# A fused attention and expert kernel: the expert layers issued in one planned order of all engines, with float32 chunks first

## The chip, the cores and the metric

The kernel runs on one core of one Trainium2 chip. The metric is the device time of one execution in microseconds (us), as the median of several runs. PE is the matrix engine (TensorE), PEld its weight loads, DVE is VectorE, ACT is ScalarE, POOL is GpSimd, and SP issues most of the DMAs.

## What is computed

Causal attention over 8 batches x 12 heads x 448 positions x 64, whose result is read as 3584 tokens of 768 numbers, and then a layer of 8 experts of which each token takes one. An expert keeps the 80 tokens with the largest gate weight; all other rows of the result are zero.

```python
def _moe_ref(x, w_gate, w1, w2, capacity):        # x (3584, 768), w1 (8, 768, 1024), w2 (8, 1024, 768)
    ...
    for e in range(E):
        ...
            keep = np.argpartition(-gw, capacity)[:capacity]
            tok_idx = tok_idx[keep]
        h = np.maximum(x[tok_idx] @ w1[e], 0.0)
        out[tok_idx] = gate_w[tok_idx, None] * (h @ w2[e])
```

## The kernel before

The first 310 us are attention, 48 pairs of heads one after another. Then comes the **tail**: the last pair, the gate of the last batch and the choice of the 80 tokens of each expert. Its steps are issued in the order of the string `TAIL`. It ends with `idx` (the rows of the chosen tokens) and `gws` (their weights) on DVE (`finish`, L956 to L969).

Then come the experts, `e` from 0 to 7. Each has two layers, and the layers of neighbours alternate: e0 layer 1, e1 layer 1, e0 layer 2, e2 layer 1, e1 layer 2, and so on. The work on one expert:

- `gather` (POOL, L1259, an indirect DMA) brings 80 rows of the attention result from `xs` in HBM into `xg`. The rows were put there by stores from `xrl` (SP, L641), the last eight of them in the tail.
- `inputs`: PE transposes `xg` into `xtp` (L1273). ACT makes the float16 high part `xh` (L1281), DVE the low part `xl` (L1282).
- The weights are loaded in **pieces** of 1.5 MB into ten buffers, `wraw`, by SP. A piece holds three **chunks** of layer 1 (128 x 1024 each) or four of layer 2 (128 x 768). 112 chunks make the 32 pieces. Ten pieces are loaded during attention, 22 later, chunk by chunk (L223).
- Each chunk is **split**: ACT makes `wh` (L1235), DVE makes `wl` = 32 w - `wh` (L1221). There are 12 buffers of `wh` and 11 of `wl`. PE then needs three float16 matmuls for each block of 128 outputs (L1303, L1305, L1306; `product`). Some chunks are left whole, in float32, with one matmul for a block (L1296): those for which `whole` is true, three in layer 1 of e0 and otherwise the last chunk of each layer, none in e6 and e7. 98 chunks are split.
- `hidden` makes `hh` (ACT) and `hl` (DVE) from layer 1's result `hp`; `outputs` copies layer 2's result `op` to `yt`, transposes it (`ytp`, PE), scales it to `yo` (ACT) and **scatters** it to `out` (POOL, L1384, an indirect DMA). A scatter waits for the one before it.

What sets the order: only PE's is the order of the code, in which the product of a whole chunk comes last in its layer (`u.order`). The order on DVE, ACT, POOL and SP is made by the framework's own scheduler from what each instruction waits for. Some waits are added by hand: no `wl` before a small memset behind the first gather (L1418) or, in later ones, before the newest `xl` (`low_after`); loads are paced by the `wl` (`PACE`).

```python
        def low(l, src, h):
            with tc.issue_after((low_after or last_of)[-1].ins):
                return nc.vector.scalar_tensor_tensor(out=l, in0=src, scalar=SW, in1=h, op0=ALU.mult, op1=ALU.subtract)
...
                        with tc.issue_after(g.ins):
                            nc.gpsimd.memset(lows[0][0][:, 0:1], 0.0)
```

Of the kernel before, what the change touches and what calls it, by code (L numbers as in the profile page):

```python
# [17 lines left out]
P = 128  # L18
# [20 lines left out]
ta ya tb yb td guard yd tc yc invert last_rows v0 v1 gA vy sA gB0 w close piece lpA r0w wy lgA r0e gB1 logA r0m r1w sB r1e  # L39
# [5 lines left out]
ROW_ENGINES = "ppappppa"  # L45


@with_exitstack
def attention_then_moe(
# [84 lines left out]
    prob = [akeep.tile([P, at], F32, name=f"prob{r}") for r in range(2)]  # L134


    HB = 3
    PH = NP // HB
    v_bufs = []
    for r in range(2):  # L140
        t = akeep.tile([P, NT, PH * P], F32, name=f"vt{r}")
        if LAST < P:
            nc.gpsimd.memset(t[0:LAST, NT - 1, :], 0.0)
        v_bufs.append(t)
# [12 lines left out]
    flipped = []  # L157
    for r in range(2):
        t = akeep.tile([P, 2, WPT], F32, name=f"PT{r}")
        flipped.append(t)  # L160
# [17 lines left out]
    PACE = 1.28  # L178

    PW = 3072
    K1, K2 = PW // F, PW // D
    PIECES = []
    for e in range(E + 1):
        if e < E:
            PIECES += [(e, 1, c, K1) for c in range(0, NC1, K1)]
        if e:
            PIECES += [(e - 1, 2, c, K2) for c in range(0, NC2, K2)]
# [9 lines left out]
    def piece():  # L199

        e, which, c, k = PIECES[len(wload)]
        x = len(wload) % (WBUF + WMORE)
        pool, bufs = (wpool, WBUF) if x < WBUF else (wmore[0], WEARLY) if x < WBUF + WEARLY else (wmore[1], WMORE - WEARLY)
        t = pool.tile([P, k, PW // k], F32, name="wraw", tag="w", bufs=bufs)
        wload.append(t)
        return t, (w1 if which == 1 else w2)[e, :, c:c + k, :]

    lows_of = []

    def load_piece(behind=None, paced=False):  # L210

        if len(wload) < len(PIECES):
            late = len(wload) - WBUF - WMORE
            t, src = piece()
            if behind is not None:
                with tc.issue_after(behind.ins):
                    nc.gpsimd.memset(t[:, 0, 0:1], 0.0)
            if not paced:
                nc.sync.dma_start(t, src)
                return  # L220
            k = t.shape[1]
            for j in range(k):
                got = nc.sync.dma_start(t[:, j, :], src[:, j, :])  # L223
                at = [f for x, f in lows_of if x <= PACE * (late + j / k)]
                if at:
                    tc.add_manual_dep(got.ins, at[-1].ins.name, mybir.DependencyInfo(
                        mybir.DependencyClass.Sync, mybir.DependencyReason.DATA), reason="paced loads")

    def piece_parts():

        got = []
        k = PIECES[len(wload)][3]
        got.append(piece())
        half = PW // k // 2

        def part(j, x):
            t, src = got[0]
            nc.sync.dma_start(t[:, j, x * half:(x + 1) * half], src[:, j, x * half:(x + 1) * half])
        return [lambda j=j, x=x: part(j, x) for j in range(k) for x in range(2)]
# [778 lines left out]

    with tc.manual_schedule():
# [125 lines left out]
        def close():  # L1145
# [11 lines left out]
        steps["close"] = close  # L1157

# [30 lines left out]
    wsplit = ctx.enter_context(tc.tile_pool(name="wsplit", bufs=1, reuse_waits="tile"))  # L1189
    ffn = ctx.enter_context(tc.tile_pool(name="ffn", bufs=2, side="right", reuse_waits="tile"))  # L1190
    ps_m = ctx.enter_context(tc.tile_pool(name="ps_m", bufs=2, space=PSUM, reuse_waits="tile"))
    ps = ctx.enter_context(tc.tile_pool(name="ps", bufs=2, space=PSUM, reuse_waits="tile"))
    HIS, LOS = 12, 11
    AHEAD = 2


    def whole(e, which, c):

        if e >= E - 2:
            return False  # L1200
        return c == NC2 - 1 if which == 2 else c >= (NC1 // 2 if e == 0 else NC1 - 1)

    SW, SX = 32.0, 8.0
    NF = F // P
    HALF = NF // 2

    PER = NC1 if NC1 * SL <= 512 else NC1 // 2

    parts_of = {}
    low_after = []  # L1210
    done = [0]

    def split_pieces(m, held=0):

        first = done[0]
        done[0] += m
        order, lows, his = [], [], []

        def low(l, src, h):
            with tc.issue_after((low_after or last_of)[-1].ins):  # L1220
                return nc.vector.scalar_tensor_tensor(out=l, in0=src, scalar=SW, in1=h, op0=ALU.mult, op1=ALU.subtract)  # L1221

        for i in range(first, first + m):
            while len(wload) <= i:
                load_piece(paced=True)
            e, which, c, k = PIECES[i]
            for j in range(k):
                src = wload[i][:, j, :]
                order.append(c + j)
                if whole(e, which, c + j):  # L1230
                    parts_of[(e, which, c + j)] = (src,)
                    continue
                h = wsplit.tile([P, PW // k], F16, name="wh", tag="wh", bufs=HIS, padded_shape=[P, max(F, D)])
                l = wsplit.tile([P, PW // k], F16, name="wl", tag="wl", bufs=LOS, padded_shape=[P, max(F, D)])
                his.append(lambda h=h, src=src: nc.scalar.activation(h, src, AF.Copy, scale=SW))  # L1235
                def split(l=l, src=src, h=h, x=i + (j + 1) / k):
                    got = low(l, src, h)
                    lows_of.append((x, got))
                    return got
                lows.append((l, split))  # L1240
                parts_of[(e, which, c + j)] = (h, l)
        for f in his[:len(his) - held]:
            with tc.issue_after(batches[-1].raised.ins):
                f()
        return order, lows, his[len(his) - held:]

    def split_now(m):
        order, lows, _ = split_pieces(m)
        for _, f in lows:
            f()  # L1250
        return order

    def gather(u):
# [5 lines left out]
        return nc.gpsimd.indirect_dma_start(  # L1259
# [4 lines left out]
    def inputs(u):  # L1264

        h = ffn.tile([P, NC1, SL], F16, name="xh", tag="xh")
        l = ffn.tile([P, NC1, SL], F16, name="xl", tag="xl")
        nw = sum(whole(u.e, 1, c) for c in range(NC1))
        w = ffn.tile([P, NC1 // 2, SL], F32, name="xw", tag="xw", bufs=1)
        for c0 in range(0, NC1, PER):  # L1270
            tp = ps_m.tile([P, PER, SL], F32, name="xtp", tag="misc")
            for c in range(PER):
                nc.tensor.transpose(tp[:, c, :], u.xg[:, (c0 + c) * P:(c0 + c + 1) * P], ident[0:SL, 0:SL])  # L1273
            part = slice(c0, c0 + PER)
            if u.e == 0:
                wp = ps_m.tile([P, PER * SL], F32, name="wp", tag="misc")
                for _ in range(5):
                    nc.tensor.matmul(wp, identb, before[:, 0:PER * SL], start=True, stop=True)
# [221 lines left out]
```

## Time and profile before

| | us |
|---|---|
| median of 3 runs (454.17 to 455.19) | 454.22 |
| the profiled execution | 456.79 |
| its span in the profile | 455.1 |
| busy in the span: PE, DVE, ACT, POOL | 428.1, 381.9, 391.2, 243.1 |
| mean granted clock of PE in the span | 0.988 |

The time of a run holds the span and what lies around it. Times in the rows below are us from the span's start. In a row of a timeline, the bracket behind an instruction is the idle time of its engine just before it and what ended that. Two instructions that follow each other directly overlap by some tens of ns, so that the mean duration of one is longer than the step from one to the next.

### The profile page before, as it was taken

How to read it: one execution, taken by the hardware profiler on the slowest of the kernel's cores; microseconds unless marked ns; L12 is line 12 of the kernel's file. 1: busy time of each engine (PE TensorE's matmuls, PEld its weight loads, DVE VectorE, ACT ScalarE, POOL GpSimd, SP SyncE). 2: the span in 40 equal slices, each digit the busy share in tenths (PEclk: the TensorE clock that was granted, in tenths of full speed). 3: DMA queues.
4: the chain of work that ended last, by engine and by line, in shares of the span. 5: the costliest groups of instructions: out<-in, count | busy, mean ns of one | idle time of the engine just before them, and what ended most of it. 6: DMA issues, size and time to landing. Idle time of an engine off the chain costs nothing. (4 is left out here: it accounts for less than half of the span.)

```text
span 455.1 us, 15784 instructions
## 1 busy us (share of the span) xinstructions
PE 428.1 (94%) x5822; PEld 334.1 (73%) x5822; DVE 381.9 (84%) x1314; ACT 391.2 (86%) x1067; POOL 243.1 (53%) x360
## 2 busy tenths in 40 slices
PE   7799999999999999999999999999798999999993
PEld 3576777777677667767767777766478999899992
DVE  6786698979979988897988989796777899999991
ACT  5999999989889899988988998885867899998971
POOL 7987638628556852853765485212450075532541
PEclk9999999999999999999999999999999899999998
DMA  8456748748556664763857574299559999999911
GB/s 260 145 207 202 255 168 274 250 135 288 194 185 227 218 219 134 262 211 126 271 192 236 164 249 160 80 325 425 221 178 337 393 400 398 399 414 412 376 30 45
DMA packets 46670, 109.95 MB, mean 242 GB/s; under 512 B 5842, under 2 KB 23250, under 8 KB 45952
## 3 DMA queue, kind: packets, MB, share of 16 engines
q1 hardware_dynamic: 45392, 105.20, 65.5%
q0 software_dynamic: 1056, 3.51, 2.3%
q8 instruction: 46, 0.75, 0.7%
q14 instruction: 32, 0.26, 0.2%
q10 hardware_dynamic: 144, 0.23, 0.1%
HBM read 85.35 MB, written 23.99 MB: 240 GB/s over the span
## 5 line engine op out<-in xcount | busy, mean ns | idle before, releaser
L449 ACT ACTIVATE prob<-ns,nb 128x192 f32<-128x192 f32 (+3 forms) x336 | 175.4, 532 | 17.6 <-DVE nb L445 16.9
L445 DVE CUSTOM_DVE_ANT_0 ns<-sp,mask 128x192 f32<-128x192 f32 (+3 forms) x336 | 134.5, 444 | 23.7 <-PE sp L426 20.1
L483 PE MATMUL tp<-ident,prob 128*128 128x128 f32 x768 | 104.4, 276 | 1.7 <-ACT PT L488 1.6
L374 POOL TENSOR_TENSOR qk<-qk,qk 128x448 f16<-128x448 f32 x94 | 96.7, 1043 | 4.2 <-DVE qk L402 1.0
L1221 DVE SCALAR_TENSOR_TENSOR wl<-wraw,wh 128x768 f16<-128x768 f32 (+1 forms) x98 | 97.1, 1061 | 1.6 <-POOL wl L1418 1.6
L506 PE MATMUL xp<-PT,vt 128*64 128x448 f32 (+3 forms) x768 | 93.6, 386 | 2.8 <-DVE xr L636 2.4
L1235 ACT ACTIVATE wh<-wraw 128x768 f16<-128x768 f32 (+1 forms) x98 | 84.3, 925 | 4.5 <-ACT yt L1369 1.7
L483 PEld LDWEIGHTS tp<-ident,prob 128*128 128x128 f32 x768 | 84.2, 141 | 4.7 <-ACT PT L488 3.4
L506 PEld LDWEIGHTS xp<-PT,vt 128*64 128x64 f32 x768 | 50.8, 136 | 46.7 <-issue 24.8
L488 ACT COPY PT<-tp 128x512 f32<-128x512 f32 x144 | 76.2, 589 | 8.3 <-PE tp L483 7.8
L426 PE MATMUL sp<-qk 64*128 64x448 f16 (+2 forms) x864 | 68.1, 297 | 4.1 <-POOL qk L374 2.8
L1306 PEld LDWEIGHTS <-wl 128*128 128x128 f16 x668 | 67.1, 100 | 3.5 <-issue 3.4
L1303 PEld LDWEIGHTS <-wh 128*128 128x128 f16 x668 | 67.6, 101 | 2.2 <-issue 2.1
L1305 PEld LDWEIGHTS <-wh 128*128 128x128 f16 x668 | 67.1, 101 | 0.1
L1384 POOL DMA_INDIRECT out<-yo,idx x8 | 40.4, 5044 | 49.2 <-ACT yo L1381 44.4
L449 ACT ACTIVATION_READ_ACCUMULATOR prob<-ns,nb 128x1 f32 x336 | 66.2, 197 | 0.0
L426 PEld LDWEIGHTS <-qk 64*128 64x128 f16 x864 | 36.5, 94 | 18.6 <-issue 3.2
L488 DVE COPY PT<-tp 64x256 f32<-64x256 f32 x144 | 43.6, 328 | 2.3
L1305 PE MATMUL hp<-xl,wh 128*128 128x80 f16 x320 | 35.8, 202 | 3.0 <-DVE xl L1282 3.0
L1306 PE MATMUL hp<-xh,wl 128*128 128x80 f16 x320 | 35.8, 202 | 2.0 <-issue 2.0
L1303 PE MATMUL op<-hh,wh 128*128 128x80 f16 x324 | 37.5, 204 | 0.0
L1306 PE MATMUL op<-hh,wl 128*128 128x80 f16 x324 | 37.4, 204 | 0.0
(187 smaller groups left out, 661.3 us busy)
## 6 DMA issues: line engine op xcount, KB each, us to landing
wraw<-w SPq DMA_DIRECT2D x48, 384.0 KB
wraw<-w SPq DMA_DIRECT2D x30, 512.0 KB
out<-mask SPq DMA_DIRECT2D x56, 192.0 KB
qk<-k_t SPq DMA_DIRECT2D x23, 448.0 KB
qk<-q_t SPq DMA_DIRECT2D x23, 448.0 KB
vt<-v_t SPq DMA_DIRECT2D x24, 384.0 KB
xs<-xr SPq DMA_DIRECT2D x42, 192.0 KB
wraw<-w SPq DMA_DIRECT2D x5, 1536.0 KB
```

What stands on the lines that cost most here:

```text
L374: sub = lambda e, o, a, b: e.tensor_tensor(out=o, in0=a, in1=b, op=ALU.subtract)
L426: nc.tensor.matmul(pr.sp[t, j], a[rows, p, queries(t)], c[rows, p, FROM[t]:FROM[t] + WIDTH[t]], start=(x == 0), stop=(x == 2))
L445: nc.vector.tensor_tensor_reduce(out=ns, in0=pr.sp[x], in1=m, scale=-1.0 / 8.0, scalar=HUGE, op0=ALU.add, op1=ALU.min, accum_out=nb)
L449: nc.scalar.activation(pr.P[:, OFF[x]:OFF[x] + w], got[0], AF.Exp, bias=got[1], scale=-1.0, accum_out=pr.sums[:, h:h + 1])
L483: nc.tensor.transpose(tp[:, i * P:(i + 1) * P], f, ident)
L488: way(part_of(pr.PT, rows, to, *todims), part_of(got[0], rows, at, *dims))
L506: nc.tensor.matmul(xp[rows, c * P:S], st["vt"][:, c, p * P + j * DH:p * P + (j + 1) * DH], pr.PT[:, j, n0:n0 + w], start=(c == 0), stop=(c ...
L1221: return nc.vector.scalar_tensor_tensor(out=l, in0=src, scalar=SW, in1=h, op0=ALU.mult, op1=ALU.subtract)
L1235: his.append(lambda h=h, src=src: nc.scalar.activation(h, src, AF.Copy, scale=SW))
L1303: nc.tensor.matmul(o, wh[:, ws], ah[:, c, :], start=(x == 0 and i % per == 0), stop=False, skip_group_check=True)
L1305: nc.tensor.matmul(o, wh[:, ws], al[:, c, :], start=False, stop=False, skip_group_check=True)
L1306: nc.tensor.matmul(o, wl[:, ws], ah[:, c, :], start=False, stop=(x == n - 1), skip_group_check=True)
```

## The change

A function `plan_experts` is added. When the program is built it simulates the expert stage with a table of costs and writes one list of operations for PE, ACT, DVE and SP together; the code then issues them in the order of this list on all engines, with the framework's own scheduling off. The waits added by hand (`issue_after`, `low_after`, `PACE`) go. A chunk that stays whole is the first of its layer and not the last, and e0 has one in layer 1 and not three, so that 100 chunks are split. The first three `wh` and the first two `wl` are made in the tail (`h0`, `h1`, `h2`, `l0`, `l1`), in buffers that lie where attention had its tiles; the order of those tiles in memory is changed for that, and the load of the tenth piece (`piece`) comes behind them. Behind the first `xtp` stand 3 matmuls that keep PE busy and not 5.

```diff
-ta ya tb yb td guard yd tc yc invert last_rows v0 v1 gA vy sA gB0 w close piece lpA r0w wy lgA r0e gB1 logA r0m r1w sB r1e
+ta ya tb yb td guard yd tc yc invert last_rows v0 v1 gA vy gB0 w close h0 sA h1 l0 h2 l1 piece lpA r0w wy lgA r0e gB1 logA r0m r1w sB r1e
...
+COST = {"hi1": 950, "hi2": 735, "lo1": 1135, "lo2": 870, "xw": 210, "xh": 460, "xl": 575, "hw": 120, "hh": 330, "hl": 400,
...
+BEGIN = {"ACT": 400, "SP": 1500, "DVE": 4300, "PE": 8900}
...
+    pe = [("xtp", 0), ("warm", 0)]
+    for e, w in layers:
+        for x, c in enumerate(order[e, w]):
+            n = len(order[e, w])
+            if w == 1 and x == n // 2 and e == 0 and E > 1:
+                pe.append(("xtp", 1))
+            if x == n // 2 and (e >= 2 if w == 1 else e == E - 1 and e > 0):
+                pe.append(("ytp", e - 2 if w == 1 else e - 1))
...
+            pe.append(("p", e, w, c))
...
+        for g in ("PE", "DVE", "ACT", "SP"):
+            if busy[g] > t:
+                continue
+            for op in queue[g][:1] if g in ("PE", "SP") else queue[g][:40]:
+                if free.get(op[0], 1) > 0 and all(
+                        d in done and done[d] + (0 if d[0] in ("ld", "got") else COST["seen"]) <= t for d in ops[op][2]):
+                    queue[g].remove(op)
...
+    def whole(e, which, c):
...
+        if e >= E - 2:
+            return False
+        return c == (NC1, NC2)[which - 1] - 1
...
+        cs = sorted(range((NC1, NC2)[which - 1]), key=lambda c: (not whole(e, which, c), c))
...
-            room = row_stack.enter_context(tc.tile_pool(name="room", bufs=1, reuse_waits="tile"))
-            room.tile([P, 7 * 512], F32, name="room")
+            pool = ctx.enter_context(tc.tile_pool(name="wsplit0", bufs=1, reuse_waits="tile"))
+            split_bufs["hi"] += [pool.tile([P, max(F, D)], F16, name=f"wh{i}") for i in range(HIS0)]
+            split_bufs["lo"] += [pool.tile([P, max(F, D)], F16, name=f"wl{i}") for i in range(LOS0)]
...
-        return c == NC2 - 1 if which == 2 else c >= (NC1 // 2 if e == 0 else NC1 - 1)
...
+    with tc.manual_schedule():
...
+            for (kind, e, *y), info in turns:
```

On DVE this is the place where the tail ends and the experts begin, in the kernel before; `gws` is the last step of the choice of tokens:

```order
L969 TENSOR_TENSOR gws_6575<-gws_6575,sv_6576 80x8
L1221 SCALAR_TENSOR_TENSOR wl<-wraw,wh 128x1024 x3
L1282 SCALAR_TENSOR_TENSOR xl<-xtp,xh 128x480
L1221 SCALAR_TENSOR_TENSOR wl<-wraw,wh 128x1024 x5
L1282 SCALAR_TENSOR_TENSOR xl<-xtp,xh 128x480
L1323 SCALAR_TENSOR_TENSOR hl<-hp,hh 128x320
L1221 SCALAR_TENSOR_TENSOR wl<-wraw,wh 128x768
L1323 SCALAR_TENSOR_TENSOR hl<-hp,hh 128x320
```

And the same place on DVE in the changed kernel:

```order
L1081 TENSOR_TENSOR gws_6587<-gws_6587,sv_6588 80x8
L1156 SCALAR_TENSOR_TENSOR wl_6338<-wraw,wh_6335 128x1024
L1156 SCALAR_TENSOR_TENSOR wl_6636<-wraw,wh_6633 128x1024
L1156 SCALAR_TENSOR_TENSOR wl_6637<-wraw,wh_6634 128x1024
L1156 SCALAR_TENSOR_TENSOR wl_6638<-wraw,wh_6635 128x1024
L1156 SCALAR_TENSOR_TENSOR wl_6639<-wraw,wh_6627 128x1024
L1156 SCALAR_TENSOR_TENSOR wl_6640<-wraw,wh_6628 128x1024
L1386 SCALAR_TENSOR_TENSOR xl<-xtp,xh 128x480
L1156 SCALAR_TENSOR_TENSOR wl_6641<-wraw,wh_6629 128x1024
L1156 SCALAR_TENSOR_TENSOR wl_6642<-wraw,wh_6630 128x1024
L1156 SCALAR_TENSOR_TENSOR wl_6643<-wraw,wh_6631 128x768
L1156 SCALAR_TENSOR_TENSOR wl_6336<-wraw,wh_6632 128x768
```

Six `wl` and not three stand ahead of the first `xl`, and four more ahead of the second one, which is further down.

On PE, the boundary between layer 1 of e1 and layer 2 of e0 in the changed kernel reads so; before, the row of the whole chunk (`hw` with `wraw`) stood behind the last split chunk of layer 2:

```order
L1443 MATMUL hp<-xh,wl_6642 128x80
L1438 MATMUL op<-hw,wraw 128x80 x6
L1441 LDWEIGHTS wh_6631
L1441 MATMUL op<-hh,wh_6631 128x80
L1442 LDWEIGHTS wh_6631
L1442 MATMUL op<-hl,wh_6631 128x80
```

The six matmuls of the whole chunk need `hw` alone; those behind them need `hh` and `hl`.

On SP, the tail's last eight stores to `xs` and the first later loads in the changed kernel; before, the eight stores stood together, and all these loads (`wraw`) behind them:

```order
L753 DMA xs<-xrl 128x384 x3
L333 DMA wraw<-w 128x1024
L753 DMA xs<-xrl 64x384
L753 DMA xs<-xrl 128x384 x2
L333 DMA wraw<-w 128x1024
L753 DMA xs<-xrl 64x384
L753 DMA xs<-xrl 128x384
L333 DMA wraw<-w 128x1024 x4
```

Two loads of 512 KB have moved in between the stores; they go to the places of the two chunks that are split in the tail.

## Rows read from the trace of the kernel before

**Rows 1.** Busy time of the engines in stretches of the end: stretch, length, then PE, PEld, DVE, ACT, POOL, clock, DMA share, GB/s.

```profile
322.00:335.00 13.00, 11.07 (x79) 6.09 (x77) 9.84 (x35) 9.56 (x17) 7.81 (x10) 0.87 0.34 107
345.00:431.00 86.00, 81.00 (x1759) 80.25 (x1756) 83.53 (x96) 78.94 (x121) 36.27 (x8) 0.98 1.03 400
```

**Rows 2.** Timeline of DVE from the last step of the tail on.

```profile
329.70 0.16 DVE L969 TENSOR_TENSOR gws<-gws,sv 80x8 f32<-80x8 f32 x1
331.42 3.50 DVE L1221 SCALAR_TENSOR_TENSOR wl<-wraw,wh 128x1024 f16<-128x1024 f32 x3 [1.57 <-POOL wl L1418]
336.43 0.66 DVE L1282 SCALAR_TENSOR_TENSOR xl<-xtp,xh 128x480 f16<-128x480 f32 x1 [1.51 <-ACT xh L1281]
343.11 0.66 DVE L1282 SCALAR_TENSOR_TENSOR xl<-xtp,xh 128x480 f16<-128x480 f32 x1 [0.34 <-ACT xh L1281]
345.86 0.49 DVE L1323 SCALAR_TENSOR_TENSOR hl<-hp,hh 128x320 f16<-128x320 f32 x1 [2.10 <-ACT hh L1322]
358.98 0.66 DVE L1282 SCALAR_TENSOR_TENSOR xl<-xtp,xh 128x480 f16<-128x480 f32 x1 [1.60 <-PE op L1306]
439.70 4.43 DVE L1221 SCALAR_TENSOR_TENSOR wl<-wraw,wh 128x768 f16<-128x768 f32 x5
```

**Rows 3.** What PE waited for from 334 to 450: us in total, times, longest.

```profile
PE hp L1305 <- DVE xl L1282: 3.0, 4, 1.1
PE hp L1306 <- issue: 2.0, 1, 2.0
```

**Rows 4.** Busy time around PE's longest wait, columns as in rows 1.

```profile
349.00:351.00 2.00, 0.03 (x2) 0.01 (x1) 2.00 (x3) 1.79 (x2) 0.00 (x0) 1.00 1.02 394
352.50:355.50 3.00, 3.00 (x35) 3.00 (x35) 3.00 (x4) 1.10 (x3) 0.00 (x0) 0.50 1.04 414
```

**Rows 5.** Timeline of PE: start of the experts, and first matmuls of two neighbouring blocks.

```profile
334.95 0.58 PE L1273 MATMUL xtp<-ident,xg 80*128 80x80 f32 x6
335.37 1.18 PE L1278 MATMUL wp<-before,identb 128*128 128x480 bf16 x5
336.38 5.48 PE L1296 MATMUL hp<-xw,wraw 128*128 128x80 f32 x48
...
342.12 0.20 PE L1303 MATMUL hp<-xh,wh 128*128 128x80 f16 x1
...
342.23 0.20 PE L1303 MATMUL hp<-xh,wh 128*128 128x80 f16 x1
```

**Rows 6.** Splits after 329.9 by shape: count, busy us, mean ns.

```profile
L1221 DVE SCALAR_TENSOR_TENSOR wl<-wraw,wh 128x768 f16<-128x768 f32 x58 | 51.4, 952 | 0.0
L1221 DVE SCALAR_TENSOR_TENSOR wl<-wraw,wh 128x1024 f16<-128x1024 f32 x40 | 46.2, 1218 | 1.6 <-POOL wl L1418 1.6
```

**Rows 7.** Timeline of ACT and of DVE in the tail, where the new splits stand.

```profile
313.93 0.27 ACT L573 COPY gs<-gp 128x128 f32<-128x128 f32 x1 [1.28 <-PE gp L567]
316.37 0.32 ACT L512 COPY xu<-xp 128x192 f32<-128x192 f32 x1 [2.17 <-PE xp L506]
...
316.72 0.42 DVE L513 COPY xu<-xp 128x256 f32<-128x256 f32 x1 [2.76 <-ACT xu L512]
```

**Rows 8.** Timeline of POOL: two of the gathers and the last three scatters.

```profile
330.19 1.07 POOL L1259 DMA_INDIRECT xg<-xs,idx  x1 [4.17 <-DVE gws L969]
333.78 1.97 POOL L1259 DMA_INDIRECT xg<-xs,idx  x1 [0.30 <-issue]
...
434.21 5.56 POOL L1384 DMA_INDIRECT out<-yo,idx  x1 [5.35 <-ACT yo L1381]
444.86 0.91 POOL L1384 DMA_INDIRECT out<-yo,idx  x1 [5.08 <-ACT yo L1381]
450.56 0.91 POOL L1384 DMA_INDIRECT out<-yo,idx  x1 [4.79 <-DMA out<-yo,idx]
```

**Rows 9.** All eight scatters together, ns min/median/max.

```profile
L1384 POOL DMA_INDIRECT out<-yo,idx x8: 912/6004/8043, 366.1 to 450.6; - x8
```

**Rows 10.** Timeline of ACT: `yo` of e6, whose second half ends last before the scatter.

```profile
443.54 1.05 ACT L1381 ACTIVATE yo<-ytp,gws 80x384 f32<-80x384 f32 x2 [2.34 <-PE ytp L1377]
```

More of the change, by code (lines that the diff above doesn't have):

```diff
@@ L208, in attention_then_moe @@
-    lows_of = []
-    def load_piece(behind=None, paced=False):
-        if len(wload) < len(PIECES):
[L213 to L227, printed above, removed]
+        return t, e, which, cs
@@ new lines, in chunk_of, with load_chunk, load_piece @@
+    def chunk_of(t, k, j):
+        return t[:, j * (PW // k):(j + 1) * (PW // k)]
+    def load_chunk(t, e, which, cs, j, x=0, parts=1):
+        w = PW // len(cs) // parts
+        nc.sync.dma_start(chunk_of(t, len(cs), j)[:, x * w:(x + 1) * w],
+                          (w1 if which == 1 else w2)[e, :, cs[j], x * w:(x + 1) * w])
+    def load_piece():
+        if len(wload) < len(PIECES):
+            t, e, which, cs = piece()
+            runs = [j for j in range(len(cs)) if j == 0 or cs[j] != cs[j - 1] + 1] + [len(cs)]
+            for a, b in zip(runs, runs[1:]):
+                w = PW // len(cs)
+                nc.sync.dma_start(t[:, a * w:b * w].rearrange("p (c f) -> p c f", f=w),
+                                  (w1 if which == 1 else w2)[e, :, cs[a]:cs[b - 1] + 1, :])
@@ L229, in piece_parts @@
     def piece_parts():
         got = []
-        k = PIECES[len(wload)][3]
+        k = len(PIECES[len(wload)][2])
         got.append(piece())
[L234 to L239, printed above, removed]
+        return [lambda j=j, x=x: load_chunk(*got[0], j, x, 2) for j in range(k) for x in range(2)]
@@ L1192, in attention_then_moe @@
     ps = ctx.enter_context(tc.tile_pool(name="ps", bufs=2, space=PSUM, reuse_waits="tile"))
[L1193 to L1200, printed above, removed]
-        return c == NC2 - 1 if which == 2 else c >= (NC1 // 2 if e == 0 else NC1 - 1)
-    SW, SX = 32.0, 8.0
     NF = F // P
     HALF = NF // 2
+    BUFS = WBUF + WMORE
     PER = NC1 if NC1 * SL <= 512 else NC1 // 2
[L1209 to L1251, printed above, removed]
     def gather(u):
@@ L1262, in gather @@
             bounds_check=N - 1, oob_is_err=False)
[L1264 to L1278, printed above, removed]
-            if nw and c0 + PER == NC1:
-                nc.scalar.activation(w[:, NC1 // 2 - nw:], tp[:, PER - nw:], AF.Copy, scale=SX * SW)
-            nc.scalar.activation(h[:, part], tp, AF.Copy, scale=SX)
-            u.xl = nc.vector.scalar_tensor_tensor(out=l[:, part], in0=tp, scalar=SX, in1=h[:, part], op0=ALU.mult,
-                                                  op1=ALU.subtract)
-        u.x = h, l, w
```

468 lines of the change are left out of this document (298 added, 170 removed).

## The prediction

> **What bounds the kernel now.** I first read the busy time by stretch [rows 1]. From 345 to 431 DVE is busy for 83.5 of 86 us, PE for 81.0, ACT for 78.9, and the DMA engines are full at 400 GB/s. No engine has much to spare there, so each gap on one of them matters only if the others can follow when it closes. Then DVE's timeline [rows 2]: between the end of `gws` (329.86) and the end of the last `wl` (444.13) it stands still five times, for 1.57 + 1.51 + 0.34 + 2.10 + 1.60 = 7.12 us, all before 359; from there on it has no gap. What ended them is to be seen in the brackets: a POOL memset, `xh` of ACT twice, `hh`, and a PE product. The work between is 114.27 - 7.12 = 107.15 us.
>
> Then PE's waits in the same stage [rows 3]: 3.0 us, in four pieces, for `xl` at the start of a layer 1, and 2.0 us in one piece, which is the stretch 349 to 351, where PE does 0.03 us of work. 1.5 us later PE is granted 0.50 of its clock (1.2 and not 2.4 GHz), for some 3.4 us [rows 4]; work at half clock takes twice as long, so this costs about 1.7 us.
>
> The end is set by two scatters in series: `yo` of e6 is ready at 444.59 [rows 10], its scatter begins at 444.86, the last one waits 4.79 us for it and begins at 450.56 [rows 8], and the span ends at 455.1. So I follow the work to `yo` of e6, behind which 10.5 us remain.
>
> **The change part by part.**
>
> *DVE's gaps.* The memset goes, and with it the 1.57. In the new order six `wl` stand ahead of the first `xl` and four before the second, so that DVE has work while it would wait for `xh`, `hh` or a PE product. There are eleven `wl` buffers; two are filled in the tail, so the tenth of these ten `wl` is the first that waits until PE gives one back. I take all five gaps as gone: 7.1 us; the lower bound is 1.57, the memset's alone.
>
> *DVE's work.* Two chunks more are split, both 128x1024, and two `wl` of that size move into the tail. Behind `gws` there are thus 98 `wl` as before, 40 and 58 [rows 6], and still 107.15 us. The last `wl` would end at 329.86 + 107.15 = 437.0.
>
> *PE's work.* Two float32 chunks of 8 blocks become float16. Float32 takes 5.48 / 24 = 0.228 us a block, three float16 matmuls 0.11 (342.12 to 342.23) [rows 5]: 16 x 0.118 = 1.9 us less. Two of five warm matmuls go: 2 x 0.24 = 0.5 less.
>
> *PE's waits.* A whole chunk needs neither `hl` nor `xl`, only `hw` or `xw`. Put first, its six or eight blocks give 1.4 or 1.8 us, more than the longest wait for `xl`, 1.1. So the 3.0 go, except in e6 and e7, which have no whole chunk. The 2.0 belong to DVE's late start, and the 1.7 of low clock to them. In all 5.0 + 1.7 + 1.9 + 0.5 = 9.1 us. PE reaches the end of e6's transposes, where ACT's `yo` starts, at 443.54 - 9.1 = 434.4, if DVE follows.
>
> *Which comes last.* DVE: e6's transposes stand behind the fourth of e7's eight chunks of layer 2. Its `wl` is four before the last: 437.0 - 4 x 0.88 = 433.5 (4.43 us for five [rows 2]); its product takes 6 x 0.11 = 0.66, and the transposes about what the six of `xtp` take, 0.58 [rows 5]: 434.8. That is behind PE's 434.4, so DVE decides, by little, and `yo` ends 1.05 later, at 435.8 and not 444.59: **8.8 us earlier**, before new costs.
>
> *The splits in the tail.* ACT has 1.28 us free before `gs` and 2.17 before `xu`, DVE has 2.76 before its `xu` [rows 7]. A `wh` of this size takes about 1.0, so one fits ahead of `gs` and two behind it; two `wl` take 1.22 + 1.14 = 2.36. All of it lies under PE's work of the last pair: cost 0. If that cover were too short by the whole of one `wl`, the choice of tokens would be 1.2 later. The tenth piece is now loaded behind the last pair's products, in a queue that is empty enough after it (0.34 of the DMA time from 322 to 335 [rows 1]): 0.
>
> *The first gather.* It ran in DVE's gap, and POOL needed 1.07 us to issue it. Now DVE runs `wl` without a break at that time. The gather at 333.78, issued beside such `wl`, took 1.97 [rows 8]. I add 0.9. All of PE's experts hang on it. Below, the bound is 0; above, it is what scatters issued beside `wl` took, up to 8.04 [rows 9]: 7.0.
>
> The Trainium skill speaks against this part: on its page "SBUF — State Buffer", section "Who interferes with whom", a DVE instruction with two inputs in SBUF contends with a GpSimd instruction that reads SBUF, and the later one is blocked until the other has finished. A `wl` has two such inputs. By that rule the gather would wait for the end of one `wl`, and the sum would be about 0.2 us worse than with the row.
>
> *Loads beside the stores and the gather.* Two loads of 512 KB now stand between the last stores to `xs`, and the next loads run from 331 instead of 335, while the gather's rows come. At 400 GB/s a load takes 1.3 us, so the gather waits between 0 and 2.6 us longer. As the DMA engines are two thirds idle there [rows 1], I take 0.7. On SP, the second of these loads holds two stores until `wl` number two is done, which is at about 316.5, long before those stores are due.
>
> *The loads' rate.* 22 pieces of 1.57 MB need 86.5 us at 400 GB/s, from 331 on at the earliest: 418, and a few us more for the start, in which buffers come free one by one. DVE works until 437. The loads do not bind; if they ran a tenth slower they would still end at 427.
>
> *The scatter of e6.* It took 0.91 us on POOL at 444.86, after DVE's last `wl` (444.13), and 5.56 at 434.21 beside them [rows 8]. Now `yo` of e6 is ready about 1 us before the last `wl` ends. I add 0.7; bounds 0 and 4.65.
>
> *A fixed order.* A late instruction now holds everything behind it on its engine. ACT has 8% to spare, DVE none, PE little. I take 0; a bound is what PE lost before to waits of this kind, 3.0.
>
> *The sum.* -8.8 + 0.9 + 0.7 + 0.7 = -6.5: the span goes from 455.1 to 448.6, and the profiled execution from 456.79 to 450.3. That execution lies 2.6 above the median of 454.22; the same step taken from the median gives **447.7 us**.
>
> **Rivals.**
>
> *Gathers as slow as scatters (the other side).* If POOL gets no turn between `wl` that follow each other without a gap, a gather takes 6.0 us, the scatters' median, or 8.0 [rows 9]. At 6.0 the first is 4.9 later; the second, which PE now needs after three chunks of e0, would be issued by 342.2, and at some 3.7 us to landing (330.19 + 1.07 to 334.95) PE waits until 345.9, where it would come at about 344.6: 1.3 more. -8.8 + 6.2 + 1.4 = -1.2: 453.0. At 8.0 the two are 7.0 and 3.3 late, -8.8 + 10.3 + 1.4 = +2.9: **457 us, slower**. The turning point is near 7 us for a gather. For it: six of eight scatters took over 4 us. Against it: a gather beside `wl` took 1.97.
>
> *The clock falls while PE waits for the first gather.* The warm matmuls end as `xtp` starts (334.95). If the gather is 1.6 later, PE stands for that long, near the 2.0 that it stood before its clock was granted by half [rows 4]. At half clock for 3.4 us it loses 1.7: 449.4, or 450.5 with a later gather.
>
> *The plan does not hold.* The order rests on a table of costs. If ACT, or a wait that the table has as 0.1 us, comes later than planned again and again, half of DVE's 7.1 us comes back elsewhere: 451.3; if all of it, the two whole chunks and the memset remain, and with the new costs nothing is left: 454.
>
> **How the numbers follow.** The forecast (446 to 449): 0.60; clock or a later gather (449 to 451): 0.16; the plan holds by half (451 to 452.9): 0.09; nothing left (452.9 to 455.6): 0.05; gathers like scatters, over 455.6: 0.05; no new costs at all (445.4 to 446): 0.05. A measurement of this kernel tells about 0.3%, 1.4 us, from no change. So faster 0.90, same 0.05, slower 0.05. The range 445.4 to 451.8 leaves out the last rivals and part of the half-held plan; the likeliest case alone is 446 to 449.
>
> **What would show it.** Right: no gap of over 0.3 us on DVE from `gws` to about 352; last `wl` near 438; PE without waits for `xl` in e1 to e5; a clock of 1.00 from 345 to 360; gather issue near 2 us; `yo` of e6 near 437.5; tail's `idx` at 329.4 as before. Wrong: a gather of over 4 us; `xtp` later than 337; `idx` later, which would mean that the splits in the tail are not hidden; waits of DVE for ACT all through the stage, which would mean that the fixed order costs what the gaps did.

## The result: slower, and the profile after

The changed kernel takes 460.27 us (median of 4 runs, 457.97 to 461.94), the kernel before beside it 454.31 (4 runs, 454.17 to 455.19): a ratio of 1.012, with an interval of 1.008 to 1.017. The forecast was 447.7, and faster. The profiled execution took 460.61 us, its span is 458.9, and the mean granted clock 0.977.

The stretches that answer to [rows 1], with one more for the start of the experts (columns as there):

```profile
322.00:335.00 13.00, 11.27 (x82) 6.19 (x80) 11.32 (x39) 8.63 (x18) 4.52 (x7) 0.87 0.87 289
345.00:431.00 86.00, 83.64 (x1808) 83.08 (x1808) 79.63 (x92) 77.13 (x118) 32.95 (x9) 0.97 0.99 378
341.00:349.00 8.00, 8.00 (x71) 7.44 (x71) 4.76 (x5) 1.84 (x4) 0.96 (x1) 0.50 0.49 141
```

In the last stretch PE is busy for 8 us and does 71 matmuls at half clock, and DVE and ACT stand still for much of it. In the first one the DMA engines are 0.87 busy and no longer 0.34.

DVE's timeline, against [rows 2]:

```profile
330.29 0.16 DVE L1081 TENSOR_TENSOR gws<-gws,sv 80x8 f32<-80x8 f32 x1
330.38 6.89 DVE L1156 SCALAR_TENSOR_TENSOR wl<-wraw,wh 128x1024 f16<-128x1024 f32 x6
342.17 0.66 DVE L1386 SCALAR_TENSOR_TENSOR xl<-xtp,xh 128x480 f16<-128x480 f32 x1 [4.90 <-ACT xh L1380]
347.17 0.96 DVE L1156 SCALAR_TENSOR_TENSOR wl<-wraw,wh 128x768 f16<-128x768 f32 x1 [1.21 <-PE hp L1443]
...
442.11 7.03 DVE L1156 SCALAR_TENSOR_TENSOR wl<-wraw,wh 128x768 f16<-128x768 f32 x8
```

The gap behind `gws` is gone. In its place stands a gap of 4.90 us ahead of the first `xl`. All gaps up to the last `wl` make 11.3 us, where they made 7.1.

The first three gathers on POOL, against [rows 8], and PE's `xtp`, against [rows 5]:

```profile
333.98 4.24 POOL L1354 DMA_INDIRECT xg<-xs,idx  x1 [7.37 <-DVE wl L1156]
338.52 0.96 POOL L1354 DMA_INDIRECT xg<-xs,idx  x1 [0.31 <-issue]
339.79 0.96 POOL L1354 DMA_INDIRECT xg<-xs,idx  x1 [0.30 <-issue]
...
340.33 1.06 PE L1370 MATMUL xtp<-ident,xg 80*128 80x80 f32 x6 [4.56 <-DMA xg<-xs,idx]
```

The first gather starts 3.8 us later than before and takes 4.24 and not 1.07. It ends at 338.22, 0.95 behind the end of DVE's six `wl` (337.27). The next two, with DVE idle, take 0.96. PE has waited 4.56 us when `xtp` starts.

What SP issued ahead of that (the stores to `xs` among loads),

```profile
310.42 7.25 SPq L343 DMA_DIRECT2D wraw<-w  x3
319.41 2.39 SPq L753 DMA_DIRECT2D xs<-xrl  x3
321.90 0.44 SPq L333 DMA_DIRECT2D wraw<-w  x1
324.13 2.04 SPq L753 DMA_DIRECT2D xs<-xrl  x3
326.91 0.33 SPq L333 DMA_DIRECT2D wraw<-w  x1
327.42 1.08 SPq L753 DMA_DIRECT2D xs<-xrl  x2
```

and the view of the stores' line for the same stretch, with the row of the 42 stores of this size that attention made, KB each and median us to landing:

```profile
DMA to landing us min/median/max: 4.9/6.8/7.9
...
xs<-xr SPq DMA_DIRECT2D x42, 192.0 KB, 2.2
```

The first row holds the tenth piece as its last load; it goes out at about 317.3 (before, the last of them was out by 311.8). Two loads stand among the stores, and the stores, as far as the trace has their landing, take 6.8 us at the median.

What PE waited for from 338 to 452, against [rows 3]:

```profile
PE xtp L1370 <- DMA xg<-xs,idx: 4.6, 1, 4.6
PE hp L1441 <- issue: 1.8, 2, 1.0
PE op L1438 <- issue: 1.2, 1, 1.2
PE op L1442 <- issue: 0.3, 1, 0.3
```

The waits for `xl` are gone, as forecast, and so are the 2.0 us. One wait at the start, of 4.6 us, nearly makes up for them (5.0 us), and 3.3 us from 399 on, for which no row names a reason, are new. The end in the timelines of ACT and POOL, against [rows 8, 10]:

```profile
447.81 1.05 ACT L1484 ACTIVATE yo<-ytp,gws 80x384 f32<-80x384 f32 x2 [1.51 <-PE ytp L1474]
449.13 0.91 POOL L1487 DMA_INDIRECT out<-yo,idx  x1 [6.95 <-ACT yo L1484]
454.40 0.91 POOL L1487 DMA_INDIRECT out<-yo,idx  x1 [4.36 <-DMA out<-yo,idx]
```

The chain of the end is as before, 4.3 us later in the span at the scatter of e6 and 3.8 at the last one. The tail itself kept its cover: the new splits filled the idle times of [rows 7], which shrank to 0.2 to 0.3 us, as on DVE:

```profile
314.82 2.53 DVE L1156 SCALAR_TENSOR_TENSOR wl<-wraw,wh 128x1024 f16<-128x1024 f32 x2
317.66 0.42 DVE L625 COPY xu<-xp 128x256 f32<-128x256 f32 x1 [0.31 <-ACT xu L624]
```

`gws` ends 0.6 later than before; the step ahead of the splits (`xu` on ACT, 310.18 against 309.23) was 0.9 late already, so that does not come from the splits.

### The profile page after: what moved, and what is told of

Read it like the earlier page. It is cut to its first block, busy times and chain, and to the rows that moved or that the text cites. A ratio compares the mean times of both kernels' runs of the same rounds, so it can differ in the third digit from the quotient of the medians.

```text
span 458.9 us, 15818 instructions
## 1 busy us (share of the span) xinstructions
PE 430.6 (94%) x5836; PEld 335.2 (73%) x5836; DVE 385.6 (84%) x1316; ACT 392.9 (86%) x1069; POOL 238.6 (52%) x359
## 5 line engine op out<-in xcount | busy, mean ns | idle before, releaser
L1156 DVE SCALAR_TENSOR_TENSOR wl<-wraw,wh 128x768 f16<-128x768 f32 (+1 forms) x100 | 99.4, 1064 | 1.7 <-PE hp L1443 1.2
L1150 ACT ACTIVATE wh<-wraw 128x768 f16<-128x768 f32 (+1 forms) x100 | 86.8, 930 | 13.3 <-PE hp L1442 8.7
L538 PE MATMUL sp<-qk 64*128 64x448 f16 (+2 forms) x864 | 69.2, 300 | 3.9 <-POOL qk L486 2.8
L1441 PEld LDWEIGHTS <-wh 128*128 128x128 f16 x684 | 69.5, 102 | 2.3 <-issue 2.3
L1443 PEld LDWEIGHTS <-wl 128*128 128x128 f16 x684 | 69.0, 101 | 0.4 <-issue 0.4
L1442 PEld LDWEIGHTS <-wh 128*128 128x128 f16 x684 | 69.0, 101 | 0.1
L1487 POOL DMA_INDIRECT out<-yo,idx x8 | 35.0, 4370 | 54.3 <-ACT yo L1484 50.0
L1441 PE MATMUL hp<-xh,wh 128*128 128x80 f16 x336 | 39.2, 205 | 1.8 <-issue 1.8
L1443 PE MATMUL hp<-xh,wl 128*128 128x80 f16 x336 | 39.2, 205 | 0.0
L1442 PE MATMUL hp<-xl,wh 128*128 128x80 f16 x336 | 39.2, 205 | 0.0
L1442 PE MATMUL op<-hl,wh 128*128 128x80 f16 x324 | 36.8, 202 | 0.3 <-issue 0.3
```

The costliest lines, as they stand in the source:

```text
L538: nc.tensor.matmul(pr.sp[t, j], a[rows, p, queries(t)], c[rows, p, FROM[t]:FROM[t] + WIDTH[t]], start=(x == 0), stop=(x == 2))
L1150: nc.scalar.activation(hi_of[y][:, 0:src.shape[1]], src, AF.Copy, scale=SW)
L1156: nc.vector.scalar_tensor_tensor(out=lo_of[y][:, 0:n], in0=src, scalar=SW, in1=hi_of[y][:, 0:n], op0=ALU.mult, op1=ALU.subtract)
L1441: nc.tensor.matmul(o, wh[:, ws], h[:, c, :], start=begin, stop=False, skip_group_check=True)
L1442: nc.tensor.matmul(o, wh[:, ws], l[:, c, :], start=False, stop=False, skip_group_check=True)
L1443: nc.tensor.matmul(o, wl[:, ws], h[:, c, :], start=False, stop=end, skip_group_check=True)
```

## The experiments

Times of one kernel spread over 1.0 to 7.6 us, in part because attention ends at another moment in each execution (`gws` at 328.7 to 330.8). So two measures stand beside each other: the ratio of times to the kernel before on the same chip, with its interval, and, from the profile, when things happen **behind the end of `gws`**. "Gather" is the start and the length of the first gather's issue; "gaps" are those of DVE from `gws` to the last `wl`. In brackets behind the median stands the time of the profiled execution. A profile is one execution and not always a typical one: those of before, of all three and of before without its gap lie 2.4 to 3.0 us over the median, while those of stores first and of 45 warm are the fastest of their kernels.

| kernel | median us (profiled) | ratio | gather | `xtp` | end of `yo` of e6 | gaps |
|---|---|---|---|---|---|---|
| before | 454.31 (456.79) | 1 | +0.33, 1.07 | +5.09 | +114.73 | 7.1 |
| after | 460.27 (460.61) | 1.012 (1.008 to 1.017) | +3.53, 4.24 | +9.88 | +118.41 | 11.3 |
| stores first | 459.49 (458.23) | 1.009 (1.007 to 1.012) | +0.56, 7.21 | +9.91 | +116.90 | 9.8 |
| piece early | 459.60 (459.60) | 1.008 (1.005 to 1.012) | +2.27, 5.49 | +9.94 | +119.94 | 12.2 |
| gap | 456.59 (456.78) | 1.002 (1.000 to 1.005) | +3.22, 1.08 | +6.15 | +115.25 | 8.1 |
| all three | 452.17 (455.12) | 0.993 (0.989 to 0.996) | +0.34, 1.08 | +4.49 | +113.85 | 6.6 |
| 45 warm | 456.45 (455.03) | 1.006 (1.003 to 1.010) | +2.96, 4.80 | +9.69 | +115.60 | 7.8 |
| before, no gap | 454.05 (456.49) | 0.999 (0.997 to 1.001) | +0.34, 1.87 | +5.26 | +114.19 | 6.6 |
| three, gap at third `wl` | 456.30 (456.14) | 0.998 (0.995 to 1.002) | +0.34, 2.89 | +7.38 | +115.80 | 8.3 |
| three, `xl` early | 453.90 (454.37) | 0.998 (0.996 to 1.001) | +0.34, 1.07 | +5.38 | +112.31 | 6.3 |
| ... and costs | 454.24 (453.14) | 0.999 (0.997 to 1.002) | +0.34, 1.07 | +4.34 | +112.29 | 5.9 |
| `xl` early, `xtp` early | 453.57 (452.92) | 0.996 (0.994 to 0.998) | +0.34, 1.07 | +4.40 | +110.52 | 4.6 |
| `xl` early, slack | 452.45 (452.03) | 0.994 (0.991 to 0.996) | +0.34, 1.08 | +4.59 | +110.91 | 4.0 |
| `xtp` early and slack | 451.78 (453.07) | 0.992 (0.989 to 0.994) | +0.34, 1.08 | +4.15 | +111.32 | 3.4 |
| the same, slack from e2 | 451.13 (450.88) | 0.994 (0.991 to 0.996) | +0.33, 1.07 | +4.11 | +109.87 | 3.1 |
| after, order mended alone | 458.96 (459.32) | 1.009 (1.006 to 1.012) | +3.20, 4.57 | +9.88 | +118.30 | 10.1 |

**Stores first, piece early, gap, all three.** Four kernels, for what makes the start late: the loads of the plan only behind the last store; the tenth piece ahead of the splits in `TAIL` (with the buffers' places in memory to match); a memset on POOL behind the first gather, for which the first `wl` waits; and all of it.

```diff
-                    load_chunk(bufs[b], *PIECES[i], j)
+                    with tc.issue_after(stores[-1].ins):
+                        load_chunk(bufs[b], *PIECES[i], j)
...
-... w close h0 sA h1 l0 h2 l1 piece lpA ...
+... w close piece h0 sA h1 l0 h2 l1 lpA ...
...
                 gather(u)
+                if u.e == 0:
+                    nc.gpsimd.memset(split_bufs["lo"][0][:, 0:1], 0.0)
```

> The changed kernel with one edit: the weight loads that the plan puts on SP's queue are issued only behind the last store of xs, as in the kernel before. Theory A (the first gather starts late because the last stores of xs share the DMA engines with the moved tenth piece and with the two loads ahead of them): POOL starts the first gather 1 to 2 us before the 333.98 of the changed kernel, xtp starts as much before 340.33, and the time is 457 to 459 us, against 460.3. Theory B (the time goes at the gather's own issue, 4.24 us against 1.07, which DVE's unbroken run of wl holds up): xtp stays within 0.5 us, since the run of wl still ends at 337.3, and the time stays at 460. Theory D (the planned order of the experts is itself slower): 460.

> The changed kernel with one edit: the buffer of the tenth piece lies where the attention lets go of it early, so that its 1.57 MB are loaded at about 311.5 us as in the kernel before, and not behind 317.3; the splits stay in the tail. Theory A: the stores of xs land sooner, the first gather starts 1.5 to 3 us before 333.98, and the time is 455 to 458.5. Theory B: the gather may start sooner, but its issue still ends when DVE's run of wl does, near 338, and the time stays within 1 us of 460.3. Theory D: 460.

> The changed kernel with one edit: the first wl of DVE behind the tail waits for a small memset that POOL does behind the issue of the first gather, so that no wl runs beside that issue (the kernel before had such a wait, at 329.70). Theory B: the gather's issue takes about 1 us and not 4.24, wherever it starts; xtp starts 1.6 to 3 us before 340.33; against it the wl of the tail's end start some 5 us later, at 335, which costs PE nothing until the first split chunk at 5.48 us x 3 behind xtp; the time is 457 to 459. Theory A: the gather still starts at 333.98, since the stores still land late, and at most the 1.6 us come back, 458.5 to 460. Theory D: 460 or more, since DVE only loses.

> The three edits together. Theories A and B together with C (the long wait of PE before xtp costs a stretch at half clock): the first gather starts at 330.5 to 331.5 and takes about 1 us, xtp starts at 335 to 336, PE runs at full clock within 2 us of it, and the time is 450 to 453 us, below the 454.3 of the kernel before. Theory D (the planned order gives nothing or costs): 454 to 458, even with the start of the experts as early as in the kernel before.

With the stores first the gather starts 3.0 us sooner, and `xtp` does not move. POOL and DVE in that kernel:

```profile
330.73 7.21 POOL L1355 DMA_INDIRECT xg<-xs,idx  x1 [4.27 <-DMA wraw<-w]
...
330.09 6.89 DVE L1157 SCALAR_TENSOR_TENSOR wl<-wraw,wh 128x1024 f16<-128x1024 f32 x6
```

The issue is longer by what it starts sooner: it ends at 337.94, again 0.95 behind DVE's run (336.98). So in all kernels in which the first gather meets the six `wl`, `xtp` starts 9.7 to 9.9 behind `gws`, wherever the gather started. Theory B's forecast came true in these two runs, and A alone does not move `xtp`; its ratios, lower by 0.003 and 0.004, lie within the intervals. The first gather with the gap alone, then with all three edits, and the stretch of the latter issue (columns as in [rows 1]):

```profile
333.68 1.08 POOL L1354 DMA_INDIRECT xg<-xs,idx  x1 [6.92 <-issue]
...
330.82 1.08 POOL L1355 DMA_INDIRECT xg<-xs,idx  x1 [4.04 <-DVE gws L1082]
...
330.82:331.90 1.08, 1.08 (x7) 0.54 (x6) 0.00 (x0) 1.08 (x2) 1.07 (x1) 1.00 0.98 364
```

The gap alone brings `xtp` to +6.15 and 3.7 us of time, 0.010 by the ratios. It has a price, which the expectation put at nothing: DVE's six `wl` start later, PE waits 2.24 us for the first `xl`, and its clock is at half from 343.2 to 346.6. Only once the gap is there do the stores count: all three edits together win 4.4 us over the gap alone, against 1.4 by the profile (both kernels ran on one chip; the profiled execution of all three is 3.0 us over its median), and the kernel is faster than before. `xtp` then starts sooner behind `gws` than before, and the time is in the expected range, but in the profiled execution PE still drops to half clock, from 340.1 to 343.5, behind a wait of 1.59 for `xl`.

The last row above also answers a rival, that the loads beside the issue make it long: the DMA engines were 0.98 busy, no `wl` ran, and it took 1.08.

**45 warm matmuls** (`*45` for `*25` at the end of `TAIL`), for the price of the clock.

> The changed kernel with one edit: 45 warm matmuls instead of 25 ahead of xtp, so that PE is busy while it waits for the late first gather (which stays late: 333.98 and 4.24 us on POOL, as nothing on POOL, SP and DVE is changed). Theory C (PE's wait of 4.6 us is what costs the clock of 341 to 349): the granted clock is 1.00 from 341 to 351, PE does in that stretch what it did at half clock in twice the time, and the time is 456 to 457, some 4 us below 460.3. Rival (the clock falls for another reason, or what PE wins there it waits for DVE's xl and wl): the clock still falls, or the waits for DVE grow by as much, and the time is 459 to 461.

```profile
341.00:349.00 8.00, 8.00 (x176) 8.00 (x176) 8.00 (x11) 5.47 (x10) 1.47 (x1) 1.00 0.87 271
```

PE is given work while it waits, `xtp` is as late as in the changed kernel, and the clock stays at 1.00: 176 matmuls in the stretch in which there were 71. `yo` of e6 comes 2.8 us sooner, and the ratio falls by 0.006, 2.7 us. So the wait itself costs the clock, and the clock about 3 us. DVE has 3.5 us of gaps less. Four of the ten times are 459.0 to 459.2, with a mean granted clock of 0.984 to 0.991 where the profiled one has 0.993; whether the clock fell at this place in those, no trace shows.

**Before, no gap** (the memset at L1418 is left out of the kernel before), as a test of theory B elsewhere.

> The kernel before with one edit: the small memset on POOL is left out for which DVE's first wl behind the tail waited, so that the three wl run beside the issue of the first gather. The stores of xs, the loads and the order are those of the kernel before. Theory B (a gather's issue lasts as long as DVE runs wl without a gap): the three wl start at 329.9, end at 333.4, and the first gather takes 3.2 us and not 1.07, from 330.2 to 333.4; xtp starts 0.5 to 1.5 us later than 334.95; DVE has 1.6 us less to wait; the time is 453.5 to 457. Rival (the long issue in the changed kernel comes from the loads and stores beside it, and not from DVE): the gather takes 1.0 to 2.0 us, and the time falls by up to 1 us, 453.3 to 454.3.

```profile
330.75 1.87 POOL L1259 DMA_INDIRECT xg<-xs,idx  x1 [4.14 <-DVE gws L969]
...
330.44 3.50 DVE L1221 SCALAR_TENSOR_TENSOR wl<-wraw,wh 128x1024 f16<-128x1024 f32 x3
```

Here B's number is wrong, and the rival's came true: the gather did not wait for the end of the three `wl` (333.94) but got in behind the first of them. The time stays the same. So the end of the run is not the rule in every case. The rival's reason, loads and stores instead of DVE, does not follow: with all three edits the loads did not make the issue long, and the next run has a long issue with the stores first.

**Three, gap at third `wl`** (`split_bufs["lo"][2]` in the memset's line), to have a run of two `wl` beside the gather in the changed order.

> The kernel with the three edits, but the small memset behind the first gather's issue holds the third wl of DVE behind the tail and not the first. So the gather begins (some 0.35 us behind the start of the first wl) beside a run of two wl and not in a gap. Theory B as it stands (the issue lasts until the run of wl is over, and 0.95 us more): the two wl end 2.3 us behind the end of gws, the gather takes about 2.8 us and not 1.08, xtp starts some 1.7 us later than in the run with the three edits (334.97 at the end of gws at 330.48), and the time is 1 to 2.5 us above its 452.2. Rival, after the run on the kernel before (1.87 us, in between the first and the second wl): the gather takes 1.6 to 1.9 us, xtp comes 0.8 us later, and the time stays within 1 us.

```profile
329.42 2.89 POOL L1355 DMA_INDIRECT xg<-xs,idx  x1 [4.18 <-DVE gws L1082]
...
329.00 2.35 DVE L1157 SCALAR_TENSOR_TENSOR wl<-wraw,wh 128x1024 f16<-128x1024 f32 x2
```

2.89 us, where B said 2.8 and the rival 1.6 to 1.9. In the changed order the issue lasts as long as the run. `xtp` comes 2.9 us later than with all three edits, and PE's clock is at half from 338.0 to 344.9. By the profile this costs 1.95 us (`yo` of e6); the ten times lie in two groups, 451.6 to 452.9 at a mean granted clock of 0.993 to 0.994 and 456.1 to 459.2 at 0.980 to 0.987, and the interval of the ratio does not tell it from the run with all three edits. The profiled execution is of the upper group; whether the issue was long in the lower one, no trace shows.

**Three, `xl` early; and costs.** What is left behind the start: is it the first wait for `xl`, or the order?

```diff
-BEGIN = {"ACT": 400, "SP": 1500, "DVE": 4300, "PE": 8900}
+BEGIN = {"ACT": 400, "SP": 1500, "DVE": 5950, "PE": 8900}
```

> The kernel with the three edits (stores first, piece early, gap) and one number of the plan changed: it takes DVE to be free for the experts at 5.95 and not at 4.3 us of its own time, as it is behind the gap. The order of DVE then has the first xl behind four wl and not behind six. Theory D1 (what is missing to the forecast comes from the first wait of PE, 1.6 us for that xl, from the half clock behind it, and from DVE's waits for a PE that is late): the wait for xl goes, the clock stays at 1.00 from 340 to 344, DVE's gaps behind the first fall from 5.0 to under 3 us, and the time is 2 to 3.5 us under the kernel with the three edits, 449 to 450.5 beside its 452.2. Theory D2 (the planned order has such gaps at any start): the gaps stay at 4 to 6 us, and the time is within 1 us of it.

> As the run before it, and twelve costs of the plan's table set to what the trace shows (hi 1000 and 790 ns, lo 1150 and 879, xw 240, xh 570, xl 590, hw 200, hh 430, hl 445, yt 570, yo 515, split 110, whole 226). Theory D2 (the order is wrong because the table is): DVE's gaps fall below 2.5 us and the time falls 1.5 us or more below the run with the start alone. Theory D1: within 1 us of that run, since the gaps come from the start of the stage and not from the table.

The wait for `xl` and the half clock go, and `yo` of e6 comes 1.5 us sooner. But DVE's gaps behind the first fall only from 5.0 to 4.7 us, and with measured costs to 4.3. By the measure that was set, D1 falls, and the table is not the cause either. The times of both are those of before. By the ratios they stand 0.6 to 0.7% above the run with the three edits, which ran on another chip. The profiles say the opposite, but that of the three edits is of an execution 3.0 us over its median, and those of these two are 0.5 over and 1.1 under theirs. The profiles show which waits went; that they won time over the three edits is not shown. What DVE waited for with `xl` early, from 330 to 446:

```profile
DVE xl L1387 <- ACT xh L1381: 4.3, 5, 1.3
DVE wl L1157 <- POOL wl L1505: 1.6, 1, 1.6
```

Five times DVE stands at an `xl` whose `xh` is late. That led to theory D3: the plan sets `xl` at the very moment at which `xh` is there by its table (0.1 us behind it), so that every delay of PE becomes a wait.

**`xtp` early; slack; both; slack from e2.** All four stand on "three, `xl` early". The slack below is that of the last two; alone it is 800, 300 and 300 ns.

```diff
-            if w == 2 and x == n // 2 and e + 2 < E:
+            if w == 2 and x == n // 2 - 2 and e + 2 < E:
...
+SLACK = {"xl": 1500, "xh": 600, "xw": 600}
...
-                        d in done and done[d] + (0 if d[0] in ("ld", "got") else COST["seen"]) <= t for d in ops[op][2]):
+                        d in done and done[d] + (0 if d[0] in ("ld", "got") else SLACK.get(op[0], COST["seen"])) <= t for d in ops[op][2]):
```

> The run with the plan's start for DVE (xl early), and xtp of the expert after next stands behind two chunks of a layer 2 and not behind four on PE; the plan then also puts xh and xl two chunks sooner. Theory D3 (DVE's and ACT's gaps at xl and xh come from the plan's rule: it puts an instruction at the very moment at which its input is there by the table, so each small delay of PE is a wait): the gaps at xl stay at 3 to 4.5 us in all, since xl moves with xtp, and the time stays within 1 us of that run. Theory D4 (they come from xtp being late on PE as such): the gaps fall below 2 us and the time by 2 us.

> The run with the plan's start for DVE, and the plan waits 0.8 us behind xh before it places xl and 0.3 us behind xtp before it places xh and xw, where it waited 0.1; by the plan itself its end does not move. Theory D3: the waits of DVE for xh (4.3 us in that run) fall to 1 to 2 us, those of ACT for xtp fall as well, yo of e6 ends 1.5 to 3 us sooner behind the end of gws than its 112.3 us, and the time is 1 to 3 us below that run. Rival (DVE's waits only move: PE or the loads bind where DVE no longer waits): the waits fall, but others of the same size take their place, and yo of e6 stays within 0.7 us of 112.3 behind gws.

> Both: xtp two chunks sooner on PE, and 1.5 us of slack behind xh for xl, 0.6 behind xtp for xh and xw. Theory D3: DVE's waits for xh below 1 us in all, yo of e6 2 to 4 us sooner behind gws than 112.3, and the time 2 to 4 us below the run with the plan's start, the lowest of all, 449 to 451. The rival of the run before (the waits only move) as there: within 0.7 us.

> The three edits, the plan's start for DVE, xtp two chunks sooner, and the slack of 1.5 and 0.6 us for the experts from the third on alone, so that the first xl stands behind four wl and not behind six. What the run with slack everywhere still lost at the start (PE waits 1.9 us for the first xl, then runs at 0.61 of its clock from 341 to 345, some 1.5 us) should come back whole if the start and the order add: yo of e6 ends at 108.5 to 110 us behind the end of gws (111.3 there), and the time is 1.5 to 3.5 us under that run, some 449. If PE or the loads bind by now, the 3.4 us are given back as waits further on: 111 to 111.5 and the same time.

Slack of 0.8 us alone takes DVE's waits for `xh` from 4.3 to 1.4 us, the ratio from 0.998 to 0.994 and `yo` of e6 from +112.3 to +110.9: D3 as expected, just short of the lower edge for `yo`. `xtp` early without slack leaves 3.0 us of gaps behind the first and ends at +110.5, a gain that D3 did not expect; more room helps as well. With both, no `xl` waits for `xh`, but `yo` comes only 1.0 us sooner and not 2 to 4: PE waits 1.9 us for the first `xl` and falls to 0.61 of its clock from 341 to 345. With slack only from e2 on that goes too. That kernel has the earliest `yo` of e6 (+109.87, inside the 108.5 to 110 expected) and the lowest median, 451.13 us beside 453.71 of before; its time was expected at some 449. By their ratios the last three kernels are not told apart, neither from each other nor from all three (0.993). All are faster than before by 0.6 to 0.8%, and than the changed kernel by about 2%.

**After, order mended alone** (`xtp` early and slack from e2, the start left as it was).

> The changed kernel with its late start left as it is (loads between the stores, the tenth piece late, six wl beside the first gather), and the mended order alone: xtp two chunks sooner, slack for the experts from the third on. If what the order costs and what the start costs are separate terms, this wins what the order was worth behind the three edits, 2 to 3 us: 457 to 458.5 against 460.3. If the order does nothing as long as the start is late (DVE has waits enough at the start to catch up in), it stays at 459.5 to 460.5.

`yo` of e6 stays (+118.30), and the ratio falls by 0.003, 1.4 us, with intervals that overlap: less than the 2 to 3 us expected if the two causes add, and perhaps nothing. The median, 458.96, lies between the two ranges expected.

## Why the prediction was wrong

Two steps failed. The one that made the kernel slower is **"The first gather"**. I took 0.9 us for it, from the gather at 333.78 that took 1.97 [rows 8], and put "gathers as slow as scatters" at 0.05. It took 4.24 us and not 1.97, and it began 3.2 us later behind `gws` than before, so that `xtp` came at +9.88 where the forecast put it at +6.7 (5.09 + 0.9 + 0.7). The row was the wrong neighbour: that gather began 0.30 behind another instruction of POOL. The first one comes after POOL has been idle, as the scatters do, and these showed what can happen. In the kernel before, POOL and DVE at two of them:

```profile
366.12 8.04 POOL L1384 DMA_INDIRECT out<-yo,idx  x1 [7.16 <-ACT yo L1381]
380.00 7.26 POOL L1384 DMA_INDIRECT out<-yo,idx  x1 [4.56 <-ACT yo L1381]
...
373.24 0.65 DVE L1282 SCALAR_TENSOR_TENSOR xl<-xtp,xh 128x480 f16<-128x480 f32 x1
...
386.36 0.88 DVE L1323 SCALAR_TENSOR_TENSOR hl<-hp,hh 128x320 f16<-128x320 f32 x2
```

They end at 374.16 and 387.26, 0.9 behind the start of the first instruction of DVE that is not a `wl`. All six scatters of over 4 us in that trace do so (the others 0.87 to 0.89). I read their lengths and not where they end. With that reading the price is no length of 6 or 8 us but the end of the six `wl`, some 6.9 + 0.95 behind `gws`, and `xtp` 2 us later. The Trainium skill (page "SBUF — State Buffer", section "Who interferes with whom") says that a DVE instruction with two inputs in SBUF contends with a GpSimd instruction that reads SBUF. I took that for a wait of one `wl`, 0.2 us more than the row; the six long first gathers waited for the whole run, others for one `wl`. That this contention is the reason is not shown here: the runs show when the issue ends, not what it waits for.

The other points, one by one:

- **Tenth piece, 0, and loads beside stores, 0.7.** Both too low: the queue was "empty enough" by a row of the kernel before, which had neither load in it. The gather could start 3.2 us later behind `gws`. In the changed kernel the run of `wl` hides this; with the gap, it is worth 1.7 us at `xtp`. The two loads weigh more than the piece: with the stores first the gather starts at +0.56, with the piece early at +2.27.
- **The clock.** A rival at 1.7 us; it came and cost some 3, by the run with 45 warm matmuls, with a wait of 4.6 us and not 1.6. (In the kernel before, the clock fell 1.2 us behind PE's wait, at 352.2, and not 1.5.)
- **All five gaps of DVE gone, 7.1 us.** This is the second step that failed. Even with the start mended 4.7 to 5.0 us of gaps remain behind the first, and 1.6 to 2.4 with slack; the first, of 1.6, is the one that the gather needs. The forecast took a list of instructions for a timeline: that ten `wl` stand ahead of two `xl` says nothing of when `xh` is there in the later experts. That "the plan does not hold" was named as a rival, at half or all of the 7.1; 6.3 to 6.6 of them were there with all three edits and with `xl` early.
- **PE's waits for `xl`** did go in e1 to e7, and the tail's splits were hidden. The scatter of e6 took 0.91 us, as before; its 0.7 did not come.

In sum, at `yo` of e6 by the profiles: forecast +107.5 (114.73 - 8.8 + 0.9 + 0.7), measured +118.4. Of the 10.9 us, 4.6 go with the three edits at the start (to 113.85), 1.5 with `xl` early (to 112.31), 2.4 with slack and `xtp` early (to 109.87), and 2.3 stay, of which 1.6 is the gap that the gather needs and which the forecast had counted as won. By the times the share of the start is larger: the ratio falls from 1.0124 to 0.9925 with the three edits, some 9 us of the 12.6 by which the forecast missed, and beyond that the edits to the order win nothing that the intervals show. Slack is clear in the waits, and in the time only against `xl` early.

For what stays, the longest wait in the last kernel's trace is one of PE within a whole chunk,

```profile
389.03 0.31 PE L1440 MATMUL op<-hw,wraw 128*128 128x80 f32 x1
390.54 1.45 PE L1440 MATMUL op<-hw,wraw 128*128 128x80 f32 x11 [1.20 <-issue]
```

which needs only `hw` and its load. The first of its twelve matmuls ran before the wait, so that neither of the two explains it; no row names what does.

## What to carry to other kernels

The issue of an indirect DMA on POOL can be held up by a run of DVE instructions with two inputs in SBUF (here 1.08 us with a gap, 2.89 to 7.21 beside a run): for each such issue in a trace, read which DVE instruction its end follows, not only how long it took. A hand-made gap that looks like waste may be there for the engine beside it, though in the kernel before its removal cost nothing (454.05 against 454.23), so try it in the order that you have. An order fixed from a cost table should place a consumer some time behind its input, since each delay is a wait for all that stands behind it; 0.8 us of slack cost nothing in the plan and took two thirds of the waits.

## What was not expected of the hardware

- The issue of an indirect DMA often lasts until DVE's run of `wl` is over and 0.95 us more (six first gathers, five beside a run of six `wl`, 6.89 us, and one beside a run of two, 2.35). In all 16 traces 89 gathers and scatters of the expert stage took over 3 us; 87 of them ended 0.78 to 0.95 us behind the last `wl` ahead of a gap of DVE or of another instruction of it. But a gather that POOL starts 0.18 to 0.31 us behind its previous instruction gets in behind the next `wl` (1.91 to 1.97 us in the kernels with the gap), and eleven issues ahead of which POOL had been idle for 2.4 to 13 us got in between two `wl` too, among them the first gather of the kernel before without its gap (1.87) and two scatters with `xl` early (1.01 and 1.08). What lets an issue in between two `wl` stays open.
- PE's clock was granted by half for 10.2 us in the three kernels in which PE waited 4.3 to 4.6 us for `xtp` (changed, piece early, order alone), from 0.5 to 1.1 us before the end of the wait on, and for 3.4 behind two waits of 0.6 and 1.6 within 5 us (all three). With warm matmuls in the wait it stayed at 1.00.
